# Sigmoid attention and a gated feed-forward block: separate transpose banks, a refitted load order, and paired seventh token tiles

## The chip, the cores and the metric

The kernel runs on one core of one Trainium2 chip. The metric is device time in microseconds (us) of one execution. The kernel before takes 422.9 us (median of three runs, 422.77 to 423.55). The names used below: PE is TensorE (PEld its weight loads), DVE is VectorE, ACT is ScalarE, POOL is GpSimd, SP is SyncE, which issues nearly all loads.

## The reference

```python
batch, n_heads, seq, head_dim = 8, 12, 448, 64        # q, k, v in float32, 0.1 * randn
scores = q @ k.T / sqrt(64) - log(448)
x = sigmoid(scores) @ v                                # 3584 tokens x 768
g = x @ w_gate                                         # 768 x 1536
h = g * sigmoid(g) * (x @ w_val)
out = h @ w_out                                        # 1536 x 768
```

## The kernel before

The kernel writes its work as a list of operations, each with an engine, an estimated duration and what it depends on. A list scheduler with a model of the loads then fixes the order of the instructions of every engine, in the program, before it runs. So an edit in one place can move instructions anywhere.

The attention is cut into 24 units of four heads (q, k and v: 448 KB each); three units make one batch entry. Per unit: cast q and k to bf16, transpose (on PE for units 0 to 5, by DMA after that), seven score bursts on a quarter array (64x64), seven sigmoids on ACT, the values products, copies to `xT`. The first three units (one batch entry, 21 sigmoids) run before there is feed-forward work. These are the parts that the change touches:

```python
ORDER = "v1 q2 q3 w0 q4 w1 w2 q5 w3 q6".split()   # order of loads; "q2" = q, k, v of unit 2, "w0" = first quarter of both weights
...
stt = [stg.tile([128, 2 * NS * D], FP32, tag=f"st{n}", name=f"st{n}") for n in range(slots["st"])]   # staging for loads
...
cast_qk(0, "q", None, [("DVE", 0, 4, 0), ("ACT", 4, NS, 0)])
tr_pe(0, 0, [("DVE", 0, 4), ("ACT", 4, NS)])       # one PSUM tile for both parts
...
cuts = [0, 5, NS] if i < QB else [0, NS]           # values product of units 0 to 2 in two parts
...
a = op("PE", 0.19 * JS, mm(w, nm, 0, JS), ...)     # first gate and value products in two parts, JS = 4
```

The output product h @ w_out of two token tiles e and o with the two halves of the inner dimension is done by seven products of six matmuls in place of eight (a Strassen-like scheme with sums on DVE). A group of two batch entries has seven token tiles of 128, so three pairs and one tile left over. Before, the seventh tile is computed the ordinary way:

```python
def f2_items(m):
    return [x for k in range(NS // 2) for x in f2_set(m, k)] + \
        [(1.0, lambda final, u=u: f2(m, u, final)) for u in (2 * NS - 2, 2 * NS - 1)]   # 12 matmuls a half-column
```

Of the kernel before, what the change touches and what calls it, by code (L numbers as in the profile page):

```python
# [27 lines left out]
class Op:  # L28
# [3 lines left out]
    def __init__(self, eng, dur, fn, deps=(), mode=("F", "F"), take=(), give=(), desc=(0, 0)):  # L32
        self.eng, self.dur, self.fn, self.mode = eng, dur, fn, mode
        self.deps = [d if isinstance(d, tuple) else (d, 0.0) for d in deps if d is not None]
        self.take = [Slot(t) for t in take]
        self.give = list(give)
        self.rank = self.t0 = self.t1 = None
        n, size = desc
        self.hold = n == 1792
        self.dma = 2.0 if n == 1792 else n / 16 * max(0.042, 0.0093 + size / 28700)  # L40
# [10 lines left out]
ORDER = "v1 q2 q3 w0 q4 w1 w2 q5 w3 q6".split()  # L51
# [7 lines left out]
VDMA = 24  # L59
VISSUE = 1.6  # L60
# [3 lines left out]
def list_schedule(ops, bufs, window):  # L64
# [34 lines left out]
    while left:  # L99
        later = []  # L100
        did = False
        for e, q in queues.items():
# [6 lines left out]
            if e == "PE" and now > 100 and mode == "Q":  # L109
                rs = [ready(o) for o in q[:NEAR] if o.mode[0] == mode]  # L110
                rs = [r for r in rs if r is not None and r <= now + STICK]
                soon = min(rs) if rs else None
# [41 lines left out]
def kernel(  # L154
# [55 lines left out]
    stt = [stg.tile([128, 2 * NS * D], FP32, tag=f"st{n}", name=f"st{n}") for n in range(slots["st"])]  # L210

    def wsum(j, c, n=1):

        x = (j - 1) * NH + c
        o = x % 4 * HW
        return stt[NEARLY + x // 4].bitcast(FP16)[:, o:o + n * HW]

# [75 lines left out]
    def load_v(i):  # L293

        b, r = divmod(i, QB)

        def fn():
            t = T["v16", i] = sb.tile([128, 2, NS, D], FP16, tag="v16", bufs=slots["v16"], name=f"v16_{i}")
            x = v[b][4 * r:4 * r + 4].rearrange("(a g) (p s) d -> a g p (s d)", a=2, s=NS)
            nc.gpsimd.dma_start(out=t[:, 0].rearrange("q s d -> q (s d)"), in_=x[0].rearrange("g p c -> (g p) c"))  # L300
            for g in range(2):
                nc.gpsimd.dma_start(out=t[64 - 64 * g:128 - 64 * g, 1].rearrange("q s d -> q (s d)"), in_=x[1, g])
        R["v16", i] = op("POOL", VISSUE, fn, take=["v16"], desc=(256, NS * D * 4))

# [40 lines left out]
    def tr_pe(i, n, parts=None):  # L345
# [4 lines left out]
        def fpe(s0, s1):  # L350
            def fn():
                if s0 == 0:
                    T["tr", i, n] = psum.tile([128, NS, 128], BF16, tag="TO", bufs=2, name="ps_tr")
# [6 lines left out]
        def fm(eng, s0, s1):  # L360
            def fn():
                if n == 0 and s0 == 0:
                    qkT_tile(i)
                cp(eng, T["qkT", i][:, n, s0:s1], T["tr", i, n][:, s0:s1])
            return fn
        for k, (eng, s0, s1) in enumerate(parts):
            a = op("PE", 0.06 * (s1 - s0), fpe(s0, s1), deps=[ins[min(k, len(ins) - 1)]],
                   take=["TO"] if s0 == 0 else [], give=R["cq", i][0].take if n and s1 == NS else [])
            if s0 == 0:
                bank = a.take  # L370
            m = op(eng, 0.1 + (0.53 if eng == "DVE" else 0.8) * (s1 - s0) / NS, fm(eng, s0, s1), deps=[a],
                   take=["qkT"] if n == 0 and s0 == 0 else [], give=bank if s1 == NS else [])
# [46 lines left out]
    def pv(i):  # L419
# [25 lines left out]
        cuts = [0, 5, NS] if i < QB else [0, NS]  # L445
# [15 lines left out]
    def f1(b, f):  # L461
# [30 lines left out]
        JS = 2 * (QB - 1)  # L492

        def product(w, nm, deps):
            deps = deps + R["w16", "w" + nm, c]
            if b or f:
# [3 lines left out]
            a = op("PE", 0.19 * JS, mm(w, nm, 0, JS), deps=xs[:JS] + deps, take=["G"])  # L500
            return op("PE", 1.14 - 0.19 * JS, mm(w, nm, JS),
                      deps=xs[:JS] + [(o, 0.19 * n) for n, (o, _) in enumerate(xs[JS:])] + [a]), a.take
# [12 lines left out]

    ev = [0]

    def f2(m, u, final=False):
        t, half = divmod(u, 2)
        end = m == B // 2 - 1 and t == NS - 1  # L520
        if end and half:
            w = DM // 4
            parts = [("A", slice(2 * w, 3 * w)), ("TO", slice(3 * w, 4 * w))]
        else:
            w = DM // 2
            parts = [("A" if final and u % 4 < 2 else "TO", slice(half * w, half * w + w))]
        a = [f2_part(m, u, final, end, n, *p) for n, p in enumerate(parts)]
        R.setdefault(("f2", m), []).extend(a)

    def f2_part(m, u, final, end, n, tag, cs):  # L530
        t, half = divmod(u, 2)
        w = cs.stop - cs.start

        def fpe():
            if half == 0:
                T["osb", m, t] = sb.tile([128, DM], FP32, tag="osb", bufs=slots["osb"], name=f"osb_{m}_{t}")
            if tag == "A":
                o = psum.tile([128, 2, 512], FP32, tag="A", bufs=2, name="ps_ol")[:, 0, 0:w]
            else:
                o = psum.tile([128, w], FP32, tag="TO", bufs=2, name="ps_o")  # L540
            T["o", m, u, n] = o
            for f in range(NF):
                nc.tensor.matmul(out=o, lhsT=T["hT", m][:, f, t * 128:(t + 1) * 128],  # L543
                                 rhs=wo16[:, f, cs], start=(f == 0), stop=(f == NF - 1))

        def fe():
            if half == n and not (end and n):
                nc.scalar.activation(out=T["osb", m, t][:, cs], in_=T["o", m, u, n], func=COPY, scale=HREC)
            else:
                nc.vector.tensor_scalar_mul(T["osb", m, t][:, cs], T["o", m, u, n], HREC)  # L550

        def fo(c, blocks, dma):
            def fn():
                for k in blocks:
                    bb, s = divmod(2 * t + k, NS)
                    rows = slice((2 * m + bb) * S, (2 * m + bb + 1) * S)
                    dma.dma_start(out=out[rows, c].rearrange("(p s) d -> s p d", s=NS)[s],
                                  in_=T["osb", m, t][64 * k:64 * k + 64, c])
            return fn
        a = op("PE", 1.95 * w / (DM // 2), fpe,  # L560
               deps=[(R["hT", 2 * m + 1, f], 0.16 * f) for f in range(NF)] + [R["wo16", f] for f in range(NF)],
               take=[tag] + (["osb"] if half == 0 else []))
        if half == 0:
            R["osb", m, t] = a.got("osb")
        e = op("ACT" if half == n and not (end and n) else "DVE", 0.1 + 0.35 * w / (DM // 2), fe, deps=[a], give=a.got(tag))
        R["o", m, u] = e
        give = R["osb", m, t] if half and (n or not end) else []
        if end and n:
            op("SP", 0.5, fo(cs, [0], nc.sync), deps=[e], give=give)
            op("ACT", 0.5, fo(cs, [1], nc.scalar), deps=[e])  # L570
        elif end:
            op("SP", 0.5, fo(cs, [0], nc.sync), deps=[e])
            if half:
                op("ACT", 0.5, fo(cs, [1], nc.scalar), deps=[e])
            else:
                op("SP", 0.5, fo(cs, [1], nc.sync), deps=[e])
        elif half == 1:
            op("SP" if final else "POOL", 1.1, fo(slice(0, DM), [0, 1], nc.sync if final else nc.gpsimd),
               deps=[e, R["o", m, u - 1]], give=give)
        return a  # L580
# [26 lines left out]

    def f2_set(m, k):

        e, o = 2 * k, 2 * k + 1  # L610
# [3 lines left out]
        def blk(t, r):  # L614
            return T["hT", m][:, r * NH:(r + 1) * NH, t * 128:(t + 1) * 128]

        def hs(f0, f1):
            bs = {x // S for t in (e, o) for x in (t * 128, t * 128 + 127)}
            return [(R["hT", 2 * m + b, f], 0.16 * (f - f0)) for b in bs for f in range(f0, f1)]

        def c(t, cols):
            return T["osb", m, t][:, cols]

        def start(final):
            full = [d for d, _ in hs(0, NF)]

            def s1():
                for n in (1, 2):
                    T["s", n, m, k] = sb.tile([128, NH, 128], FP16, tag=f"S{n}", bufs=slots["S"],
# [12 lines left out]
        def product(n, lhs, rhs, deps, final):  # L642
            tag = "A" if final and n % 2 else "TO"

            def fn():
# [4 lines left out]
                for x in range(NH):  # L650
                    nc.tensor.matmul(out=T["p", m, k, n], lhsT=lhs()[:, x], rhs=rhs(x),  # L651
# [8 lines left out]
        def store(t, deps, give, final):  # L660
            dma = nc.sync if final else nc.gpsimd

            def fn():
                for x in (0, 1):
                    bb, s = divmod(2 * t + x, NS)
                    rows = slice((2 * m + bb) * S, (2 * m + bb + 1) * S)
                    dma.dma_start(out=out[rows].rearrange("(p s) d -> s p d", s=NS)[s],  # L667
                                  in_=T["osb", m, t][64 * x:64 * x + 64])
            op("SP" if final else "POOL", 1.1, fn, deps=deps, give=give)

        def step1(final):
# [4 lines left out]
            def fn():  # L676
                for t in (e, o):
                    if final:
                        T["osb", m, t] = staging("osf")[:, 0:DM]
                    else:  # L680
                        T["osb", m, t] = sb.tile([128, DM], FP32, tag="osb", bufs=slots["osb"], name=f"osb_{m}_{t}")
# [8 lines left out]
        def step3(final):  # L690
# [3 lines left out]
            add("c11", 2, (e, lo), (e, lo), [C["u2"]])  # L694

# [4 lines left out]
        def step5(final):  # L700
# [3 lines left out]
            P[5].give = C["s1"].take  # L704

        def step6(final):
            product(3, lambda: blk(e, 1), lambda x: wo16[:, NH + x, hi], [C["s4"]], final)
            add("c12", 3, (e, hi), (e, hi), [C["u4"]])
            store(e, [C["c11"], C["c12"]], C["p1"].take[:1], final)
# [182 lines left out]
```

## Time and profile before

| | kernel before |
|---|---|
| time, span of the profiled run | 422.9 us, 421.4 us |
| PE busy | 412.1 us (98%) |
| DVE, ACT, POOL busy | 54%, 52%, 31% |
| PE full from | 48 us to the end |
| from PE's last matmul to the end of the span | 3.55 us (span less 416.70 + 1.15) |

The lines that carry the reading are in the prediction. Read them so: where PE is full, only the number of matmuls counts; where it is not full (here the first 48 us), follow the waits in order of time; at the end, count what comes after the last matmul.

### The profile page before, as it was taken

To read this page: it belongs to the slowest core of one execution; us is meant where nothing else is said; L and a number is where in the kernel's file an instruction comes from. 1 tells how busy PE (TensorE), PEld (TensorE's weight loads), DVE (VectorE), ACT (ScalarE), POOL (GpSimd) and SP (SyncE) were. 2 spreads that over 40 slices of the span, in tenths; PEclk is the share of its full clock that TensorE was granted. 3 is DMA by queue.
4 is the path that set the end of the run, shared out by engine and by line. 5 is a ranking of instruction groups with operands and counts; after the bars stand their busy time and mean duration, and the time that the engine had idled before them with its cause. 6 is when DMAs were issued, how large, how long until landed. Compare 5 with 4: busy or idle time off the path is not lost.

```text
span 421.4 us, 7959 instructions
## 1 busy us (share of the span) xinstructions
PE 412.1 (98%) x3215; PEld 208.0 (49%) x3217; DVE 229.5 (54%) x401; ACT 218.8 (52%) x292; POOL 130.0 (31%) x194
## 2 busy tenths in 40 slices
PE   8989899999999999999999999999999999999996
PEld 3444444444445554554554544545445545555564
DVE  3444444467676744554465564555455474673773
ACT  5997578766771155455645446544745542112000
POOL 1887845766331231414304314224100001000000
PEclk9999999999999999999999999999999999999999
DMA  8999979997871284474663745746301103021054
GB/s 273 379 376 374 375 208 340 308 321 209 221 230 54 75 207 91 146 178 106 165 165 76 185 56 195 176 87 188 59 2 37 39 2 75 2 75 35 4 148 116
DMA packets 64628, 66.97 MB, mean 159 GB/s; under 512 B 35536, under 2 KB 60752, under 8 KB 64592
## 3 DMA queue, kind: packets, MB, share of 16 engines
q1 hardware_dynamic: 62704, 59.29, 49.0%
q0 software_dynamic: 1728, 7.08, 6.5%
q8 instruction: 25, 0.41, 0.4%
q10 hardware_dynamic: 160, 0.10, 0.1%
q14 instruction: 11, 0.09, 0.1%
HBM read 47.19 MB, written 11.01 MB: 138 GB/s over the span
## 4 chain that ended last, share of the span: by engine, by line
PE 89%; DMA 9%; SPq 1%; POOL 0%; issue 0%; DVE 0%; POOLq 0%
PE ps_g L472 25%; PE ps_v L472 23%; PE ps_o L651 16%; PE ps_sc L397 8%; PE ps_pv L432 6%; DMA st<-in_moe_w_val_dram 4%; DMA st<-in_q_dram 4%; PE ps_ol L651 4%; PE ps_vl L472 3%; PE ps_o L543 2%; PE ps_ol L543 2%; SPq L261 1%; PE ps_tr L355 0%; POOL src L231 0%; DVE osb L550 0%
## 5 line engine op out<-in xcount | busy, mean ns | idle before, releaser
L414 ACT ACTIVATE pt<-ps_sc,sbiast 128x896 f16<-128x896 f32 x168 | 159.1, 1006 | 29.1 <-PE ps_sc L397 29.1
L472 PE MATMUL ps_g<-xT,wg 128*128 128x448 f16 x576 | 124.3, 353 | 0.5 <-DVE t L482 0.4
L478 ACT ACTIVATE s<-ps_g 128x448 f16<-128x448 f32 x96 | 52.2, 544 | 123.8 <-PE ps_g L472 122.8
L472 PE MATMUL ps_v<-xT,wv 128*128 128x448 f16 x504 | 109.7, 353 | 0.0
L482 DVE TENSOR_TENSOR t<-ps_g,s 128x448 f16<-128x448 f32 x96 | 59.9, 624 | 91.3 <-ACT s L478 91.0
L472 PEld LDWEIGHTS <-wg 128*128 128x128 f16 x576 | 54.7, 98 | 55.4 <-issue 8.1
L472 PEld LDWEIGHTS <-wv 128*128 128x128 f16 x576 | 52.3, 98 | 58.3 <-issue 15.9
L488 DVE SCALAR_TENSOR_TENSOR hT<-ps_v,t 128x448 f16<-128x448 f32 x84 | 52.4, 624 | 34.6 <-PE ps_v L472 33.6
L231 POOL CAST src<-st 128x896 bf16<-128x896 f32 (+1 forms) x43 | 39.8, 927 | 100.6 <-DMA st<-in_q_dram 67.2
L397 PE MATMUL ps_sc<-qkT 64*64 64x448 bf16 x672 | 51.3, 360 | 1.8 <-ACT pt L414 1.3
L231 POOL CAST v<-st 64x448 f16<-64x448 f32 (+1 forms) x72 | 41.4, 575 | 25.8 <-issue 15.7
L651 PEld LDWEIGHTS <-hT 128*128 128x128 f16 x360 | 35.2, 98 | 25.4
L667 POOL DMA_DIRECT2D out_dram<-osb x32 | 16.7, 526 | 90.4 <-DVE osb L656 90.4
L432 PE MATMUL ps_pv<-pt,v 64*64 64x448 f16 x672 | 37.1, 350 | 0.4 <-ACT pt L414 0.4
L229 DVE CAST xT<-ps_pv 128x448 f16<-128x448 f32 x40 | 23.5, 620 | 24.0 <-PE ps_pv L432 24.0
L656 DVE SCALAR_TENSOR_TENSOR osb<-ps_o,osb 128x384 f32<-128x384 f32 x56 | 30.2, 552 | 6.3 <-PE ps_o L651 6.3
L651 PE MATMUL ps_o<-wo,hT 128*128 128x384 f16 x168 | 31.9, 326 | 0.0
L397 PEld LDWEIGHTS <-qkT 64*64 64x64 bf16 x672 | 14.9, 105 | 31.1 <-issue 27.3
L432 PEld LDWEIGHTS <-v 64*64 64x64 f16 x672 | 19.6, 107 | 14.3 <-issue 3.4
L651 PE MATMUL ps_o<-st,s 128*128 128x384 f16 x120 | 22.8, 326 | 0.0
L651 PE MATMUL ps_o<-st,hT 128*128 128x384 f16 x120 | 22.8, 326 | 0.0
L651 PEld LDWEIGHTS <-s 128*128 128x128 f16 x144 | 14.1, 98 | 10.2
(45 smaller groups left out, 202.5 us busy)
## 6 DMA issues: line engine op xcount, KB each, us to landing
st<-in_q_dram SPq DMA_DIRECT2D x24, 448.0 KB, 4.3
st<-in_v_dram SPq DMA_DIRECT2D x24, 448.0 KB, 5.5
st<-in_k_dram SPq DMA_DIRECT2D x23, 448.0 KB, 4.8
out_dram<-osb POOLq DMA_DIRECT2D x36, 192.0 KB, 3.2
st<-in_moe_w_gate_dram SPq DMA_DIRECT2D x12, 384.0 KB, 9.1
st<-in_moe_w_val_dram SPq DMA_DIRECT2D x12, 384.0 KB, 8.8
st<-in_moe_w_out_dram SPq DMA_DIRECT2D x12, 384.0 KB, 6.8
out_dram<-st SPq DMA_DIRECT2D x16, 192.0 KB, 2.7
```

Of the source, the lines that this page charges most:

```text
L229: nc.vector.tensor_copy(out=o, in_=i)
L231: nc.gpsimd.tensor_copy(out=o, in_=i)
L397: nc.tensor.matmul(out=sc[64 * (g ^ a):64 * (g ^ a) + 64, a, 0:S].rearrange("k (s p) -> k s p", s=NS), lhsT=kT[r, s, 64 * g:64 * g + 64], ...
L414: nc.scalar.activation(out=pt, in_=T[("sc",) + key][:, :, 0:S], func=SIGM, bias=sb_t, scale=qkscale)
L432: nc.tensor.matmul(out=T["pv", i, a][64 * g:64 * g + 64, :], lhsT=T["v16", i][r, a, s, :], rhs=T["pt", i, s][r, a, :], start=(s == 0), sto ...
L472: nc.tensor.matmul(out=T[nm, b, f], lhsT=w[c][:, j, ff * 128:(ff + 1) * 128], rhs=T["xT", b, j], start=(j == 0), stop=(j == KC - 1))
L478: nc.scalar.activation(out=t, in_=T["g", b, f], func=SIGM)
L482: nc.vector.tensor_tensor(out=t, in0=T["g", b, f], in1=T["s16", b, f], op=MULT)
L488: nc.vector.scalar_tensor_tensor(out=T["hT", m][:, f, o * S:(o + 1) * S], in0=T["v", b, f], scalar=HSC, in1=T["t1", b, f], op0=MULT, op1=MULT)
L543: nc.tensor.matmul(out=o, lhsT=T["hT", m][:, f, t * 128:(t + 1) * 128], rhs=wo16[:, f, cs], start=(f == 0), stop=(f == NF - 1))
L651: nc.tensor.matmul(out=T["p", m, k, n], lhsT=lhs()[:, x], rhs=rhs(x), start=x == 0, stop=x == NH - 1)
L656: C[name] = op("DVE", 0.45, lambda: nc.vector.scalar_tensor_tensor(out=c(*dst), in0=T["p", m, k, n], scalar=HREC, in1=c(*other), op0=MULT, ...
```

## The change

Its intent: start the sigmoid row earlier, take away two holes before PE is full, and replace the four ordinary seventh tiles by two pairs, which takes 12 of 96 matmul equivalents away. Two groups share a pair: POOL copies the seventh tile of the first group (`keep`), so that it stays until the seventh tile of the second group is there.

```diff
-ORDER = "v1 q2 q3 w0 q4 w1 w2 q5 w3 q6".split()
+ORDER = "v1 q2 q3 w0 q4 w1 q5 w2 q6 w3".split()
-        self.dma = 2.0 if n == 1792 else n / 16 * max(0.042, 0.0093 + size / 28700)
+        self.dma = 2.0 if n == 1792 else n / 16 * max(0.042, 0.003 + size / 24600)
...
-    stt = [stg.tile([128, 2 * NS * D], FP32, tag=f"st{n}", name=f"st{n}") for n in range(slots["st"])]
+    stage = stg.tile([128, slots["st"], NST], FP32, tag="st", name="st")
+    stt = [stage[:, n] for n in range(slots["st"])]
+    kept = stage.bitcast(FP16)[:, NEARLY:, 4 * HW:].rearrange("p a (b t) -> p a b t", t=128)
...
-        cuts = [0, 5, NS] if i < QB else [0, NS]
+        cuts = [0, 2, 5, NS] if i < QB else [0, NS]
...
+            for j in range(0, KC, 2):        # first gate and value products in three parts
+                a = op("PE", 0.38, mm(w, nm, j, j + 2), ...)
...
+    def keep(m):
...
+            return lambda: nc.gpsimd.tensor_copy(
+                out=kept[:, 3 * r:3 * r + 3],
+                in_=T["hT", m][:, r * NH:(r + 1) * NH, (NS - 1) * 128:].rearrange("p (a b) t -> p a b t", b=2))
...
+        last = k == NS // 2
+        e, o = ((m - 1, NS - 1), (m, NS - 1)) if last else ((m, 2 * k), (m, 2 * k + 1))
...
-    tr_pe(0, 0, [("DVE", 0, 4), ("ACT", 4, NS)])
-    cast_qk(0, "k", None, [("DVE", 0, 3, 0), ("POOL", 3, NS, 1)])
-    tr_pe(0, 1, [("DVE", 0, 3), ("DVE", 3, NS)])
+    tr_pe(0, 0, [("DVE", 0, 4), ("ACT", 4, NS)], split=True)        # a bank for each part
+    cast_qk(0, "k", None, [("DVE", 0, 1, 0), ("DVE", 1, 3, 0), ("POOL", 3, NS, 1)])
+    tr_pe(0, 1, [("DVE", 0, 1), ("DVE", 1, 3), ("DVE", 3, NS)], tag="G")
...
-        return [x for k in range(NS // 2) for x in f2_set(m, k)] + \
-            [(1.0, lambda final, u=u: f2(m, u, final)) for u in (2 * NS - 2, 2 * NS - 1)]
+        return [(0.0, lambda final: keep(m))] * (1 - m % 2) + \
+            [x for k in range(NS // 2 + m % 2) for x in f2_set(m, k)]
```

Cut out: the old `f2` and `f2_part`, which go; the stores of the last pair, which are cut by half-columns and issued by SP and ACT; PE's fill matmuls at the start, which now read `wide` alone and no longer wait for the identity; and small changes of the scheduler's constants and of its order rules.

## The prediction

> **What bounds the kernel now.** I read the page first, then busy time by stretch, then the first 62 us in order of time, then the chain of work that ended last. The page's first lines, and of the stretches the two around the place where TensorE fills up and one late one (stretch, length, busy time of PE, PEld, DVE, ACT, POOL, granted clock, DMA share, GB/s):
>
> ```profile
> span 421.4 us, 7959 instructions
> PE 412.1 (98%) x3215; PEld 208.0 (49%) x3217; DVE 229.5 (54%) x401; ACT 218.8 (52%) x292; POOL 130.0 (31%) x194
> ```
>
> ```profile
> 36.00:48.00 12.00, 10.50 (x98) 4.92 (x97) 5.38 (x9) 7.74 (x10) 8.97 (x12) 1.00 1.06 375
> 48.00:60.00 12.00, 12.00 (x110) 5.49 (x107) 6.38 (x11) 8.24 (x12) 8.41 (x12) 1.00 0.79 231
> 350.00:400.00 50.00, 50.00 (x302) 27.22 (x300) 29.14 (x52) 9.19 (x18) 1.36 (x3) 1.00 0.16 40
> ```
>
> From 48 us to the end TensorE never waits: the list of waits on PE between 48 and 410 us comes back empty. There only the number of matmuls counts. Before 48 us other things set the pace, so I read that part in order of time (start, duration, engine, line, instruction, idle time before it and who ended it):
>
> ```profile
> 6.03 0.48 ACT L227 COPY qkT<-ps_tr 128x384 bf16<-128x384 bf16 x1 [1.40 <-DVE qkT L229]
> 6.99 7.51 ACT L414 ACTIVATE pt<-ps_sc,sbiast 128x896 f16<-128x896 f32 x8 [0.48 <-PE ps_sc L397]
> 14.98 11.99 ACT L414 ACTIVATE pt<-ps_sc,sbiast 128x896 f16<-128x896 f32 x13 [0.48 <-PE ps_sc L397]
> ...
> 31.05 1.29 PE L472 MATMUL ps_g<-xT,wg 128*128 128x448 f16 x6 [0.35 <-DVE t L482]
> ...
> 43.59 0.93 POOL L231 CAST src<-st 128x896 bf16<-128x896 f32 x1 [0.43 <-DMA st<-in_q_dram]
> 44.58 0.56 PE L355 MATMUL ps_tr<-idn,src 128*128 128x128 bf16 x7 [1.47 <-POOL src L231]
> ```
>
> Three things are to be seen. From 6.99 to 26.97 us ScalarE runs 21 sigmoids nearly back to back (7.51/8 = 0.94 us each); everything up to the first gate product hangs on when that row starts, and it has one hole of 0.48 us. At 31.05 PE waits for a PSUM bank. At 44.58 PE waits 1.47 us for the cast of unit 5's q, which waited for its load: the queue is full until 48 us (375 GB/s), and q5 stands behind six loads of weights.
>
> **What the Trainium skill says.** "PSUM — Partial Sum Buffer", Terms, says that two engines on one bank and quadrant at once is an error, so users of a bank have to be serialised. The trace agrees: ScalarE's copy of three transposes waits 1.40 us, until VectorE's copy from the same bank is through. "TensorEngine Tiling (Array Packing)", Key Properties: changing the tiling mode drains TensorE. The trace agrees: in the chain a six-matmul product takes 1.14 us, and 1.24 after a burst of 64x64 products. So I counted stretches of 64x64 work in the built programs: 81 before, 81 after. "TensorE: Matmul & The Clock Gate", Part 1, gives about 3.4 us of activity before the full clock; here the first fill matmuls load weights 0.43 us apart and later ones 0.21. "Perfetto Trace Analysis", Identifying the Most-Contended Engine, warns that matmul busy time misleads; therefore I work below with counts times pitch.
>
> **The change, part by part.**
>
> *Seventh token tiles.* Before, each of the four token groups computes it classically: 8 half-columns of 12 matmuls, 84 of 384 columns and 24 of 192. After, tiles of two groups make a pair with seven products of six: 2 x 42 = 84 of 384 columns. The chain gives the pitch:
>
> ```profile
> 378.20 1.95 PE ps_ol L543 x12
> 396.37 1.95 PE ps_ol L651 x12
> ```
>
> Both forms cost 1.95/12 = 0.1625 us a matmul. Before: 96 equivalents = 15.6 us; after 84 = 13.65. That is **-1.95 us**, all on PE while it is saturated. It adds 4 copies of 128x768 on POOL (0.82 us each by the weight casts; POOL is idle 69%), and some 8 sums (0.55 us) plus 14 scaled adds (0.55 us) on VectorE, about 12 us on an engine that idles 192 us: beside other work. In the built program the copies stand well ahead of their readers.
>
> *The end.* Before, the last piece is 192 columns: VectorE 0.36 us, then 48 KB stores. After, it is 384 columns and 96 KB stores on two queues:
>
> ```profile
> 417.89 0.36 DVE L550 TENSOR_SCALAR osb<-ps_o 128x192 f32<-128x192 f32 x1 [0.63 <-PE ps_o L543]
> ```
>
> ```profile
> out_dram<-osb SPq DMA_DIRECT2D x2, 96.0 KB, 2.3
> out_dram<-osb ACTq DMA_DIRECT2D x2, 48.0 KB, 2.0
> ```
>
> VectorE's add of 384 columns takes 0.55 (row of the scaled adds), so +0.19; landing +0.25. **+0.45 us.**
>
> *Separate banks for the first unit's transposes.* With its own bank ScalarE waits for TensorE alone (the built program shows this), not for VectorE's copy. The transposes it needs start about 4.9 to 5.1 us; with the drain the copy can start near 5.4 instead of 6.03. First sigmoid near 6.4 instead of 6.99: -0.6 us. *Values product in three parts:* a score burst can now stand between the parts, where before twenty products stood in front of the second score burst of unit 1 and made the 0.48 us hole: -0.5. Together the sigmoid row ends near 25.9 instead of 26.97, **-1.1 us**, if every input is there. I checked the loads: the last of unit 2 is in at 15.4, and its scores are not needed before 19; unit 4's k is cast by 28.74, needed near 28.8 (tight).
>
> *The first gate and value products* come in three parts, and ScalarE now takes the gate's sigmoid after one score sigmoid, not two. The bank wait at 31.05 should shrink or move; PE reaches the second gate product near 29.3 instead of 31.05, but one score burst (0.5 us) then comes after it rather than before. Net of the 1.1 above: **-0.15 us**.
>
> *Order of loads.* q5 goes ahead of w2, and q6 ahead of w3. One piece lands about every 1.05 us (casts of w2 at 36.87, 37.89, 38.95), an attention piece every 1.2. So q5 and k5 are cast by about 39, and PE needs them near 41: **the 1.47 us stall goes**. The price: w2 lands 3.6 us later. Its gate half would be cast near 43.5 and its value half near 46.4; my walk along the new PE order needs them near 46.6 and 49.6. w3 would be cast by 53.5 and 56.6, needed near 56.5 and 58. Margins are 1.4 to 3 us. So **-1.47 us**.
>
> The refitted load model and the earlier "stay with attention" rule only reorder; the count of mode changes is equal, at most one less in the saturated part: 0 to -0.2, taken as **-0.1**.
>
> Sum: -1.95 + 0.45 - 1.1 - 0.15 - 1.47 - 0.1 = **-4.3 us**. 422.9 - 4.3 = **418.6 us**, 1.0% faster.
>
> **The rivals.**
> 1. *Startup gain eaten by the loads.* Until 48 us the queue runs full, and no byte is removed. If PE comes 2.7 us earlier to weights that come 3.6 us later, the 1.47 us stall returns in front of w2 or w3, or at unit 4's transposes. For it: 375 GB/s, the tight k4. Against: margins of over 1 us. The time would then be 420 to 420.5.
> 2. *The end becomes VectorE's.* The last 168 matmuls (27.3 us) are now all output work, with 3 or 4 sums and 7 adds a pair, about 6 us of VectorE per 6.8 us of PE. If an add chain falls behind, PE waits for banks. Against: the three pairs before run just so from 400 to 413 us without a gap. Worth +0.5 to +1.
> 3. *A false dependency.* Staging becomes one tile, and the kept tiles lie in its slots. If readers of weight sums had to wait for POOL's copies, PE would stall in mid kernel. Against: in the built program PE's waits in the output products are of the same kinds and number as before (3 on POOL in both).
> 4. *Larger gain:* the earlier fill (its wait for the identity, built at 1.34, is gone; zeros are there at 1.13) brings the full clock earlier and the first transposes pass faster, another 0.2 to 0.4 us.
>
> **Range and chances.** The matmul count is sure to 0.1 us. The startup sum of 2.7 us I trust to about 1 us, more downwards; the end to 0.3. Rivals 1 to 3 lean slower. So 417.5 to 420.3 should hold it 8 times in 10. Faster by over 2% would need 414.4, some 4 us more than anything I find; slower by over 2% needs a new stall of 12 us in a saturated kernel. Chances: 0.02, 0.97, 0.01.
>
> **What would show each step.** Right: first sigmoid near 6.4 us and 21 of them without a hole until about 25.9; no PE wait on POOL's cast of q5 near 43; PE full from about 46; 12 output matmuls fewer in equivalents; last VectorE add of 0.55 us and some 4.0 us from the last matmul to the end (3.55 now). Wrong: PE idle before w2 or w3 products between 44 and 58 us, waits on VectorE among the last 168 matmuls, or PE waiting for POOL's kept copies. What would break the prediction is such a wait in the saturated part, where every microsecond counts in full.

## The result, and the profile after

The changed kernel is correct. It took 420.54 us (median of six runs, 419.33 to 421.38), the kernel before 422.88 (six runs, 422.58 to 423.55). The ratio is 0.9941, with a 95% interval of 0.9923 to 0.9959. A ratio here is the mean time of one kernel's fast runs over that of the other's of the same rounds, so not quite the ratio of the medians. It is faster by 0.6%, but 420.54 lies above the predicted range of 417.5 to 420.3, and 2.34 us were gained where 4.3 were expected.

The page's first two lines after, and the stretch in which PE fills up (columns as in the prediction):

```profile
span 419.0 us, 7945 instructions
PE 410.4 (98%) x3194; PEld 205.1 (49%) x3194; DVE 237.7 (57%) x420; ACT 217.5 (52%) x290; POOL 133.3 (32%) x196
```

```profile
36.00:48.00 12.00, 12.00 (x116) 5.76 (x114) 6.59 (x12) 8.67 (x11) 9.98 (x13) 1.00 1.06 376
```

The hole between 36 and 48 us is gone (10.50 before, 12.00 now). The first sigmoid, the sigmoid row and the way to the second gate product, in order of time:

```profile
5.35 0.48 ACT L231 COPY qkT<-ps_tr 128x384 bf16<-128x384 bf16 x1 [0.75 <-PE ps_tr L348]
6.31 3.70 ACT L408 ACTIVATE pt<-ps_sc,sbiast 128x896 f16<-128x896 f32 x4 [0.48 <-PE ps_sc L391]
10.52 6.39 ACT L408 ACTIVATE pt<-ps_sc,sbiast 128x896 f16<-128x896 f32 x7 [0.50 <-PE ps_sc L391]
17.50 9.25 ACT L408 ACTIVATE pt<-ps_sc,sbiast 128x896 f16<-128x896 f32 x10 [0.60 <-PE ps_sc L391]
...
29.50 0.56 PE L348 MATMUL ps_tr<-idn,src 128*128 128x128 bf16 x7 [0.68 <-POOL src L235]
...
30.70 0.56 PE L348 MATMUL ps_tr<-idn,src 128*128 128x128 bf16 x7 [0.26 <-POOL src L235]
31.10 1.30 PE L466 MATMUL ps_g<-xT,wg 128*128 128x448 f16 x6
```

ACT's copy now waits for PE alone, and the first sigmoid starts at 6.31, as predicted (6.4). But two new holes of 0.50 and 0.60 us stand in the row, which therefore ends at 26.75 (17.50 + 9.25), 0.2 us earlier than before and not 1.1. PE then waits 0.94 us for the casts of unit 4's q and k, which wait for their loads (the last part of that q landed at 28.36 us, its cast began at 28.51), and the second gate product starts at 31.10 where I had 29.3. Yet the stall that the new load order was to remove is gone. The cast and the transposes of unit 5's q:

```profile
38.42 0.93 POOL L235 CAST src<-st 128x896 bf16<-128x896 f32 x1 [0.46 <-DMA st<-in_q_dram]
...
42.81 0.55 PE L348 MATMUL ps_tr<-idn,src 128*128 128x128 bf16 x7
```

At the end, PE's last product, and DVE's last add:

```profile
413.66 1.14 PE L599 MATMUL ps_o<-st,hT 128*128 128x384 f16 x6
...
414.83 0.56 DVE L604 SCALAR_TENSOR_TENSOR st<-ps_o,st 128x384 f32<-128x384 f32 x1 [0.42 <-PE ps_o L599]
```

PE ends at 414.80, 3.05 us earlier than before (4.75 expected), and 4.2 us follow it (419.0 - 414.80; 3.55 before, 4.0 expected). So the mechanism of each part is visible. In the prediction's own terms, all that is missing is missing at the start: the row of sigmoids ends 0.85 us late (26.75 for 25.9), the second gate product starts 1.8 us late (31.10 for 29.3), and PE's end is late by no more than that (1.7 us, 4.75 - 3.05).

### The profile page after: what moved, and what is told of

Read it like the earlier page. It is cut to its first block, busy times and chain, and to the rows that moved or that the text cites. A ratio compares the mean times of both kernels' runs of the same rounds, so it can differ in the third digit from the quotient of the medians.

```text
span 419.0 us, 7945 instructions
## 1 busy us (share of the span) xinstructions
PE 410.4 (98%) x3194; PEld 205.1 (49%) x3194; DVE 237.7 (57%) x420; ACT 217.5 (52%) x290; POOL 133.3 (32%) x196
## 3 DMA queue, kind: packets, MB, share of 16 engines
q0 software_dynamic: 1632, 6.69, 6.3%
## 4 chain that ended last, share of the span: by engine, by line
PE 90%; DMA 6%; DVE 1%; ACT 1%; SPq 0%; issue 0%; POOL 0%; POOLq 0%
PE ps_g L466 26%; PE ps_v L466 23%; PE ps_o L599 18%; PE ps_sc L391 8%; PE ps_pv L426 7%; PE ps_ol L599 5%; DMA st<-in_k_dram 4%; PE ps_vl L466 3%; DMA st<-in_v_dram 3%; ACT pt L408 0%; SPq L265 0%; PE ps_tr L348 0%; DVE t L476 0%; DVE hT L585 0%; POOL src L235 0%
## 5 line engine op out<-in xcount | busy, mean ns | idle before, releaser
L599 PEld LDWEIGHTS <-hT 128*128 128x128 f16 x384 | 37.6, 98 | 27.2
L614 POOL DMA_DIRECT2D out_dram<-osb x34 | 17.7, 525 | 93.6 <-DVE osb L604 93.5
L604 DVE SCALAR_TENSOR_TENSOR osb<-ps_o,osb 128x384 f32<-128x384 f32 x63 | 34.0, 551 | 6.2 <-PE ps_o L599 6.2
L599 PE MATMUL ps_o<-st,s 128*128 128x384 f16 x138 | 26.2, 326 | 0.0
L599 PE MATMUL ps_o<-st,hT 128*128 128x384 f16 x138 | 26.2, 326 | 0.0
L599 PEld LDWEIGHTS <-s 128*128 128x128 f16 x168 | 16.4, 98 | 11.8
```

Source lines behind the costliest of these rows:

```text
L599: nc.tensor.matmul(out=T["p", m, k, n], lhsT=lhs()[:, x // 2, x % 2], rhs=rhs(x), start=x == 0, stop=x == NH - 1)
L604: C[name] = op("DVE", 0.45, lambda: nc.vector.scalar_tensor_tensor(out=c(*dst), in0=T["p", m, k, n], scalar=HREC, in1=c(*other), op0=MULT, ...
L614: dma.dma_start(out=out[rows, cols].rearrange("(p s) d -> s p d", s=NS)[s], in_=T[("osb",) + t][64 * x:64 * x + 64, cols])
```

## The experiments

My theories for what is missing: **J**, the loads land at other times in each execution, and the changed kernel's start hangs on them; **L**, unit 4's transposes wait for loads in every execution; **C**, the pairs' added work disturbs PE. The rival of J is **S**: something in the changed program makes its loads late every time.

### 1. The same kernels again

No edit. Kernels `a_...` are made from the changed kernel, `b_...` from the one before.

> The changed kernel once more, nothing edited. What is open: in its first profile the pieces of q, k and v landed up to 1.9 us later than in the kernel before (q4 cast at 28.5 us against 26.6), although the same bytes moved, and ScalarE's row of 21 sigmoids got two holes (0.50 and 0.60 us). Theory J (jitter: one of the 16 DMA engines is held up now and then, and a load lands when its slowest engine is through): this profile will have other landing times, q4's cast anywhere from 26.6 to 28.6 us, and the times scatter over some 2 us around 420.5. Rival S (something in the changed program makes the loads late every time): q4's cast again at 28.5 within 0.3 us and both holes again.

> The kernel before once more, for its profile. Theory J: its landings move too, q4's cast between 26.6 and 28.6 us; because its sigmoid row starts 0.7 us later it may hide more of it. Rival S: q4's cast at 26.6 within 0.3 us again, as in the first profile of it.

> The changed kernel a third time, as the measure for its neighbours on the chip. Theory J (landings and the opening of TensorE's clock differ from execution to execution, not from program to program): median between 419.3 and 420.6, scatter 1.2 to 2.1 us, and its profile shows other landing times than the first two. Rival S: 420.5 within 0.3 and q4's cast at 28.5 as in the first profile.

| run | us, median (all runs) | ratio to before, interval |
|---|---|---|
| first measurement | 420.54 (419.33 to 421.38) | 0.9941 (0.9923, 0.9959) |
| a_again | 419.35 (418.87 to 420.06) | 0.9911 (0.9895, 0.9927) |
| a_again2, on another chip than a_again | 419.94 (419.69 to 421.71) | 0.9933 (0.9913, 0.9953) |
| b_again (one run) | 423.49 | |

The sigmoid row of a_again, and its transposes of unit 4 with the second gate product:

```profile
6.23 10.19 ACT L408 ACTIVATE pt<-ps_sc,sbiast 128x896 f16<-128x896 f32 x11 [0.51 <-PE ps_sc L391]
16.63 9.25 ACT L408 ACTIVATE pt<-ps_sc,sbiast 128x896 f16<-128x896 f32 x10 [0.21 <-PE ps_sc L391]
...
28.59 0.56 PE L348 MATMUL ps_tr<-idn,src 128*128 128x128 bf16 x7 [0.64 <-POOL src L235]
...
29.86 0.56 PE L348 MATMUL ps_tr<-idn,src 128*128 128x128 bf16 x7 [0.33 <-POOL src L235]
30.26 1.30 PE L466 MATMUL ps_g<-xT,wg 128*128 128x448 f16 x6
```

This is the row that I had predicted: no hole but one of 0.21, and its end at 25.88 (25.9 predicted). The same program gave 26.75 in its first profile. What differs is set beside each other here, all from the profiles. "k of unit 1, first and last" is when the first and when the last of the 16 parts of that load landed, counted in the trace from the first landing of all; all other times count from the start of the span.

```
                         before  b_again  b_neworder | changed  a_again  a_again2
k of unit 1, first         4.05     3.89     4.07    |   4.09     3.73     3.90
k of unit 1, last          5.77     4.86     6.69    |   6.54     5.08     5.84
unit 4's q, first part    24.73    24.69    24.99    |  24.82    24.51    24.81
unit 4's q, last part     26.43    27.21    27.46    |  28.36    27.46    26.98
unit 4's q cast starts    26.58    27.36    27.61    |  28.51    27.60    27.12
TensorE's full clock from  5.57     5.76     6.89    |   4.98     4.75     6.38
first sigmoid              6.99     7.03     7.16    |   6.31     6.23     6.69
row of 21 sigmoids ends   26.97    27.00    27.50    |  26.75    25.88    26.32
unit 4's transposes wait                             |   0.94     0.97     0.17
second gate product                                  |  31.10    30.26    29.73
time of that execution   423.29   423.49   422.41    | 420.82   420.06   419.76
```

The first part of k of unit 1 lands within 0.4 us of the same moment everywhere. Its last part comes 1.0 to 2.6 us after it, and that differs from execution to execution, in the kernel before as in the changed one. For unit 4's q it is 1.7 to 3.5 us. A load is usable only when its last part is there: the cast of that q starts 0.14 to 0.15 us after it in all six. Rival S falls: a_again and a_again2 show other landings with the same program, and the kernel before can be late too. In the changed kernel the time follows the start of the second gate product closely: time less that start is 389.72, 389.80 and 390.03 us. Between these three executions the start moves by 1.37 us and the time by 1.06. The first profile caught it late. Only the profiled execution of each measurement can be looked at so. And a_again and a_again2 ran on different chips: whether the chip has a part in their medians was not tested.

A second source shows in the first PE work. Ten transposes at 4.6 us took 0.91 us in the first profile, 0.90 in a_again and 1.25 in a_again2, and the first sigmoid came at 6.31, 6.23 and 6.69. "TensorE: Matmul & The Clock Gate", Part 1, of the Trainium skill says that the clock opens by a free-running window, so at another moment in each run. The clock records, which the trace files keep, agree (table above). In the eight profiles of kernels with the split banks in which the full clock came after 6.3 us, the first sigmoid starts at 6.69 to 6.85 us; in the seven in which it came by 5.1 us, at 6.17 to 6.41. That is some 0.5 us.

### 2. The order of loads, undone and alone

```diff
 # a_oldorder, in the changed kernel          # b_neworder, in the kernel before: the reverse edit
-ORDER = "v1 q2 q3 w0 q4 w1 q5 w2 q6 w3".split()
+ORDER = "v1 q2 q3 w0 q4 w1 w2 q5 w3 q6".split()
```

> The changed kernel with the old order of loads (w2 ahead of q5, w3 ahead of q6). My prediction gave the new order 1.47 us, all of it a TensorE wait on the cast of q5: then this one takes 1.5 us longer than the changed kernel (422.0). Rival (the order only moves a wait that TensorE would make up elsewhere, because the bytes limit the start anyway): within 0.5 us of the changed kernel.

> The kernel before with nothing but the new order of loads. Prediction: 1.5 us less than the kernel before (421.4), the TensorE wait of 1.47 us at 44.6 us gone. Rival: the wait comes back in front of the products of the third weight quarter (44 to 58 us), and the time stays within 0.5 us of the kernel before.

Measured on one chip with a_again: a_oldorder 421.60 us (420.75 to 421.69), 2.25 more than a_again; b_neworder 422.01 (421.87 to 422.41), 1.14 less than the kernel before (423.15; ratio 0.9973, 0.9959 to 0.9986). In b_neworder the wait on unit 5's q is gone from the list of waits, and PE is full between 36 and 48 us (12.00), although its row ended 0.5 us later than in the other profiles of the kernel before (table above). Its stretch from 36 to 48 us:

```profile
36.00:48.00 12.00, 12.00 (x130) 5.80 (x126) 6.04 (x10) 9.09 (x12) 9.84 (x13) 1.00 1.06 377
```

From the second gate product to the end of the span it took 388.93 us, the kernel before 390.35 and 390.52. So the order alone is worth 1.1 us by the times and 1.4 to 1.6 us in that stretch; 1.47 was predicted. The way back is no clean measure. PE's waits after 60 us in a_oldorder (line waited for: us in total, times, longest):

```profile
PE ps_g L466 <- DVE t L476: 1.2, 2, 0.9
PE ps_sc L391 <- ACT pt L408: 1.1, 1, 1.1
PE ps_v L466 <- DVE hT L482: 0.2, 1, 0.2
```

Of these 2.5 us (0.74 in a_again) 0.93 is the wait near 120 us that section 6 explains, and 1.09 is a wait of one score burst at 60.44 us. The scheduler, given the old order, also placed other instructions elsewhere: by line and tile, 170 of 3192 matmuls stand in another place than in a_again. That it causes the new waits is not shown. It did so in b_neworder too (426 of 3215), but there PE has no wait after 60 us, as in the first profile of the kernel before. So b_neworder is the better test of the step, though not a perfectly clean one.

### 3. Loads made lighter, transposes made later

a_halfw0 and a_halfv keep every instruction in its place and move fewer bytes. Their outputs are wrong, which doesn't matter for the times. a_m7 and a_m15 tell the scheduler to expect the transposes of unit 3 and later 0.7 or 1.5 us later (those of unit 3 kept their place among their neighbours, those of unit 4 moved).

```diff
 # a_halfw0: each load of the first weight quarter moves one of its two row blocks
-                out=T[nm, c, j2],
+                out=T[nm, c, j2][:, 0:1 if c == 0 else 2],
 # a_halfv: v of units 0 to 4 moves one of its two halves, and the cast reads that half twice
-                    out=T["st_" + nm, i][:, :, s0:s1]...
+                    out=T["st_" + nm, i][:, 0:1 if nm == "v" and i < 5 else 2, s0:s1]...
 # a_m7 (a_m15: 1.5)
-MARGIN = 0.0
+MARGIN = 0.7
-                   deps=[(ins[min(k, len(ins) - 1)], -MARGIN if i > QB else 0.0)],
+                   deps=[(ins[min(k, len(ins) - 1)], -MARGIN if i >= QB else 0.0)],
```

> The changed kernel with the same instructions in the same order; only the six loads of the first weight quarter move half their bytes (the result is wrong on purpose). Everything behind them, unit 4's q and k first, lands some 3 us earlier. Theory L (the missing microsecond of my startup sum is the wait of unit 4's transposes for their loads, 0.97 us in the repeated profile): both waits go, the second gate product starts near 29.3 us instead of 30.26, and the time is 1.0 us under the changed kernel's 419.35 of the last session, about 418.4. Rival A (ScalarE's sigmoid row paces that stretch anyway, the wait only fills a gap): the time stays at 419.3.

> The changed kernel with the same instructions in the same order; only the loads of v of units 0 to 4 move half their bytes (the result is wrong on purpose), so that what stands behind them lands up to 2.4 us sooner. Theory L (loads cost the start its missing gain): no hole in the sigmoid row after unit 1, no wait of unit 4's transposes, second gate product near 29.3 us, and the time 0.7 to 1.0 us under the changed kernel beside it, with less scatter. Rival (a wait further on takes it back): within 0.3 us of it.

> The changed kernel with the load model of the scheduler told to expect unit 4's and later transposes 0.7 us later. In the built program the transposes of unit 4's q now stand behind the last value parts, those of its k three groups further on. Theory L: the waits shrink from 0.97 us to under 0.3 and the time falls by 0.6 to 1.0 us against the changed kernel, to about 418.5. Rival A: no gain, 419.3, because scores of unit 4 then reach ScalarE later.

> The same with 1.5 us: the transposes of unit 4's q stand behind the second gate product and a burst of scores. Theory L: no wait is left even where loads land late, so the time is as with 0.7 us, 418.4, and scatters less than the changed kernel (which scattered 2.05 us over six runs and 1.2 over four). Rival A: slower than with 0.7 us by 0.3 us or more.

| run | us, median (all runs) | ratio, interval |
|---|---|---|
| a_halfw0 | 419.82 (418.59 to 420.75) | 0.9909 (0.9885, 0.9933) |
| a_m7 | 419.99 (419.51 to 420.87) | 0.9919 (0.9899, 0.9940) |
| a_m15 | 420.96 (420.13 to 421.88) | 0.9942 (0.9920, 0.9965) |
| a_halfv, beside a_again2 | 419.95 (418.84 to 420.80) | 0.9922 (0.9904, 0.9940) |

a_halfv's way to the second gate product:

```profile
27.96 0.55 PE L348 MATMUL ps_tr<-idn,src 128*128 128x128 bf16 x7
28.35 0.54 PE L466 MATMUL ps_v<-xT,wv 128*128 128x448 f16 x2
28.73 0.55 PE L348 MATMUL ps_tr<-idn,src 128*128 128x128 bf16 x7
29.14 1.30 PE L466 MATMUL ps_g<-xT,wg 128*128 128x448 f16 x6
```

The mechanism of theory L is confirmed: with lighter loads both waits vanish in both kernels, the row has no hole over 0.21 us, and PE is there at 29.14 (29.3 predicted; 29.61 in a_halfw0, whose clock opened late, at 6.73 us). But the time did not follow. The median equals that of a_again2 (419.94), and six runs still scatter over 1.96 us. So L is a miss as an account of the time. Two readings remain. The loads ahead of the first v (k of unit 0, q and k of unit 1) and the clock's opening were not touched and still scatter. And a part is given back: from the second gate product to the end of the span a_halfv took 388.36 us and a_halfw0 388.39, the changed kernel 387.90, 387.94 and 388.27, with PE waiting for DVE after 60 us for 0.94 and 1.0 us against 0.54, 0.74 and 0.85. What makes all of the 2 us of scatter stays open.

a_m7 has no wait at the transposes in its profile, but PE then waits 0.26 us for the bank of the gate product; in a_m15 that wait is 0.65 us, since the second gate product stands straight behind the first values. Neither ran beside the changed kernel on its chip, nor did a_halfw0; by their ratios a_m7 is no better than the changed kernel, and a_m15, 0.97 us over a_m7 beside it, no better either. The rival's "no gain" holds; the way is another than it named, since the transposes trade their wait for one at the bank.

### 4. The first unit: one bank, two parts

```diff
 # a_nosplit
-    tr_pe(0, 0, [("DVE", 0, 4), ("ACT", 4, NS)], split=True)
+    tr_pe(0, 0, [("DVE", 0, 4), ("ACT", 4, NS)])                    # and k's partition as before
 # a_twopart
-        cuts = [0, 2, 5, NS] if i < QB else [0, NS]
+        cuts = [0, 5, NS] if i < QB else [0, NS]
```

> The changed kernel with the first unit's transposes back in one bank for q and the old partition for k. Prediction: ScalarE's copy waits for VectorE's again and the first sigmoid starts near 7.0 us instead of 6.2 to 6.85 (seen in six profiles), the row of 21 sigmoids ends 0.6 us later, and the time is 0.6 us over the changed kernel. Rival (in most executions the loads of units 1 to 4 set the end of the row and the start behind it, not the first sigmoid): the row starts later but the time differs by less than 0.3 us.

> The changed kernel with the values product of the first units in two parts again (five slices, then two). Prediction: twenty products stand ahead of a burst of unit 1's scores, the hole of 0.48 us in the sigmoid row is back, and the time is 0.5 us over the changed kernel. Rival (loads set the end of that stretch): less than 0.2 us.

a_nosplit took 419.66 us (419.30 to 420.52, ratio 0.9905), a_twopart 419.63 (419.14 to 419.90, ratio 0.9901), both as fast as the changed kernel or faster. ACT's copy and row in a_nosplit, then the row in a_twopart:

```profile
5.69 0.48 ACT L231 COPY qkT<-ps_tr 128x384 bf16<-128x384 bf16 x1 [1.03 <-DVE qkT L233]
6.66 19.52 ACT L408 ACTIVATE pt<-ps_sc,sbiast 128x896 f16<-128x896 f32 x21 [0.48 <-PE ps_sc L391]
```

```profile
6.47 7.50 ACT L408 ACTIVATE pt<-ps_sc,sbiast 128x896 f16<-128x896 f32 x8 [0.48 <-PE ps_sc L391]
14.36 11.86 ACT L408 ACTIVATE pt<-ps_sc,sbiast 128x896 f16<-128x896 f32 x13 [0.39 <-PE ps_sc L391]
```

Each shows its mechanism: with one bank the copy waits for DVE again (1.03 us), and with two parts the hole after eight sigmoids is back (0.39). Yet the rows end at 26.18 and 26.22 us, within the 25.88 to 26.75 of the changed kernel. Worth of the split banks in the start of the row: 0.35 to 0.43 us (6.66 against 6.31 and 6.23; the full clock came at 4.64, 4.98 and 4.75 us in these), not 0.6, and worth in time: none that can be seen. Here the rivals hold. With one bank the row of 21 has no hole at all. The profiled execution of a_nosplit was the slowest of its six (420.52): in it PE waits 1.07 us for DVE at 119.76 us, which section 6 explains.

### 5. The seventh tiles the old way, and another end

a_classic7 and a_classic7b (the same kernel twice) take back the old `f2` for the seventh tiles and drop `keep`; all else is as changed. a_tail cuts the very last product in two:

```diff
 # a_classic7, a_classic7b
-        return [(0.0, lambda final: keep(m))] * (1 - m % 2) + \
-            [x for k in range(NS // 2 + m % 2) for x in f2_set(m, k)]
+        return [x for k in range(NS // 2) for x in f2_set(m, k)] + \
+            [(1.0, lambda final, u=u: f2(m, u, final)) for u in (2 * NS - 2, 2 * NS - 1)]
 # a_tail: step 7 of the last pair as two products of 192 columns, each with its add and its stores
+            if end:
+                return last_halves(final)
```

> The changed kernel with the seventh token tiles computed the old way, by 96 products of twelve, and the old ending; the rest as changed. My prediction: 1.95 us of matmuls come back and 0.45 us at the end go, so 1.5 us more than the changed kernel, about 420.9. Rival: the additional VectorE and GpSimd work of the pairs costs TensorE waits, then the difference is under 1 us; or the end costs less than I said, then it is nearer to 2 us.

> The seventh tiles the old way once more. Measured from the start of the second gate product to the end of the execution, its first profile took 388.63 us, those of the changed kernel 387.90, 387.94 and 388.27: the pairs gain 0.6 us there and not the 1.5 of my prediction. Expected again: 388.6 within 0.3, and no TensorE wait at 119 us.

> The changed kernel with its very last product cut in two halves of 192 columns, each with its own add and 48 KB stores. TensorE ends 0.18 us later (12 x 0.096 against 6 x 0.1625), the last add takes 0.36 us instead of 0.56, and the stores land some 0.4 us sooner after it (3.15 us from the last add to the end before, 3.6 after). Expected: from TensorE's last matmul to the end 3.6 us instead of 4.15, net 0.4 us less. Rival: the two additional stores queue up behind the earlier ones and the gain is under 0.1 us.

a_classic7 took 420.72 us (ratio 0.9937, 0.9915 to 0.9959), a_classic7b 420.26 (0.9927, 0.9914 to 0.9939). Two things follow.

First, these two kernels hold everything of the change but the pairs, and gain 0.63% and 0.73% of 423 us, that is 2.7 and 3.1 us. Their spans say the same: 418.5 and 418.6 us against 421.4 and 421.6 of the kernel before. My sum for those parts was 1.1 + 0.15 + 1.47 + 0.1 = 2.8 us. So these parts were right as a sum.

Second, from the second gate product to the end they took 388.63 and 388.92 us, the changed kernel 387.90, 387.94 and 388.27. The pairs gain 0.74 us there (mean 388.78 less 388.04), not 1.5: the rival of a_classic7 ("under 1 us") holds. By the times alone nothing of it is seen: the mean ratio of three measurements of the changed kernel is 0.9928, that of these two 0.9932, and they did not run beside each other.

The end of a_classic7 has the lines of the kernel before (last matmul to end 418.5 - 414.92 = 3.6 us); the changed kernel has 4.2, 4.14 and 4.24. So the end costs 0.64 us, not 0.45: the add takes 0.20 more (0.56 against 0.36), and from there to the end of the span it is 3.61, 3.55 and 3.64 us against 3.15 before, 0.45 where I had 0.25. a_tail was a miss: 420.13 us (ratio 0.9910), which cannot be told from the changed kernel, and in its profile 4.5 us follow the last matmul (418.8 - 414.33), more than the 4.2 that it was to cut. The issuing of its stores (SPq and ACTq lines are the time in which a queue issues) and its last add:

```profile
411.57 4.28 SPq L614 DMA_DIRECT2D out_dram<-st  x5
411.57 4.58 ACTq L614 DMA_DIRECT2D out_dram<-st  x5
...
414.36 0.36 DVE L682 SCALAR_TENSOR_TENSOR st<-ps_ol,st 128x192 f32<-128x192 f32 x1
```

Each queue issues five stores in a row, which lasts until 415.85 and 416.15, over a microsecond past the end of the last add (414.72). The smaller pieces are ready sooner and stand in line behind the issues of the others, as the rival said.

### 6. The copies that are kept

In the changed kernel PE waits for DVE at 119 to 120 us, in each of its three profiles (0.24, 0.44 and 0.55 us); neither profile of the old tiles has that wait. There, in the changed kernel's first profile:

```profile
117.56 0.75 DVE L582 TENSOR_TENSOR s<-s,hT 128x768 f16<-128x768 f16 x1
117.85 1.14 POOL L541 COPY st<-hT 128x768 f16<-128x768 f16 x1
118.23 1.17 DVE L585 TENSOR_TENSOR hT<-hT 128x768 f16<-128x768 f16 x1
...
119.99 1.29 PE L466 MATMUL ps_g<-xT,wg 128*128 128x448 f16 x6 [0.24 <-DVE t L476]
```

The sums take 0.75 and 1.17 us (0.54 or 0.55 alone) beside POOL's cast of k, which runs until 117.90, and its copy, and the copy takes 1.14 (0.82 alone). "SBUF — State Buffer", Who interferes with whom, of the Trainium skill says that a VectorE instruction with two inputs in SBUF contends with a GpSimd instruction that reads SBUF. This agrees.

```diff
 # a_keepact, a_keepact2, a_keepact3 (one kernel); a_km7 adds the edit of a_m7
-            return lambda: nc.gpsimd.tensor_copy(
+            return lambda: nc.scalar.copy(
-            R["kept", m, r] = op("POOL", 0.95, fn(r), ...)
+            R["kept", m, r] = op("ACT", 0.85, fn(r), ...)
```

> The changed kernel with the four copies of 128x768 (hidden rows kept for the pairs) on ScalarE instead of GpSimd. In the profiles of the changed kernel VectorE's two sums beside the first copy take 0.75 and 1.17 us where they take 0.55 elsewhere, and TensorE then waits 0.24 to 0.44 us for VectorE at 119 us; with the old seventh tiles that wait is absent. Theory C (GpSimd's copy and VectorE's sum hold each other up): the sums take 0.55 again, the wait at 119 us is gone, the time 0.3 us less. Rival V (it is just the added VectorE work): the wait stays.

> The copies on ScalarE once more, beside the changed kernel on one chip. Theory C (GpSimd's copies hold VectorE's sums up and TensorE then waits 0.24 to 0.54 us at 119 us): 0.4 to 0.8 us less than the changed kernel beside it. Rival: the gain of a_keepact was landing luck, then within 0.2 us of it.

> The pairs with the copies on ScalarE. Theory C (the collision with GpSimd ate part of the 1.95 us, the longer end 0.64 of them): from the second gate product to the end it takes 387.6 within 0.2 again (387.54 and 387.67 so far), 1.0 us less than the old form beside it, and the time is 1.0 to 1.3 us less. Rival: the old form is as fast within 0.5 us, so the pairs are worth nothing once their end is paid for.

> Copies on ScalarE, and the transposes of unit 4 placed later as in a_m7. If the waits of the transposes (0.2 to 1.0 us) and the wait at 119 us add up, it takes 0.3 to 0.8 us less than a_keepact2, about 418.2. Rival: the transposes only trade their wait for one on VectorE's gate product (0.26 us in a_m7), then it equals a_keepact2 within 0.3 us.

| run | us, median (all runs) | ratio, interval |
|---|---|---|
| a_keepact | 418.82 (418.29 to 419.53) | 0.9885 (0.9865, 0.9904) |
| a_keepact2, beside a_again2 | 419.08 (418.67 to 419.92) | 0.9905 (0.9889, 0.9920) |
| a_keepact3, beside a_classic7b | 419.26 (418.67 to 419.51) | 0.9899 (0.9886, 0.9913) |
| a_km7, beside a_again2 | 420.14 (418.57 to 420.38) | 0.9919 (0.9900, 0.9937) |

Copies on ACT are faster than either form beside which they ran: 0.86 us less than the changed kernel on one chip (419.94), 1.0 less than the old tiles on another (420.26), and on three chips about 1% less than the kernel before. From the second gate product to the end they took 387.54, 387.67 and 387.42 us. The wait at 119 us is gone in all three profiles. But theory C holds only in part. The same place in a_keepact:

```profile
115.73 0.92 DVE L579 TENSOR_TENSOR s<-hT 128x768 f16<-128x768 f16 x1
...
117.57 0.90 DVE L585 TENSOR_TENSOR hT<-hT 128x768 f16<-128x768 f16 x1
...
118.76 1.14 PE L599 MATMUL ps_o<-wo,hT 128*128 128x384 f16 x6
...
119.73 1.30 PE L466 MATMUL ps_g<-xT,wg 128*128 128x448 f16 x6
```

Two of the sums are still slow, now beside POOL's casts of q, k and v (the kernel before has sums of 0.73 and 1.17 us beside such casts, too, and PE does not wait there). The three sums ahead of that gate product (L579, L582, L585) settle what the wait is. With the old tiles they take 2.20 us together, in both profiles:

```
                       changed  a_again  a_again2  a_nosplit | a_keepact  a_keepact2  a_keepact3
the three sums            2.47     2.66      2.77       3.29 |      2.36        2.67        2.44
what they take over 2.20  0.27     0.46      0.57       1.09 |      0.16        0.47        0.24
PE's wait after them      0.24     0.44      0.55       1.07 |      none        none        none
```

With the copies on POOL, PE's wait is what the sums take over 2.20 us, to within 0.03 us, in these four profiles and in seven further ones. But the copy is not all of it. In a_again and a_again2 the first sum alone takes 1.12 and 1.23 us; it starts when POOL's cast of k has begun and the copy has not. With the old tiles it started 0.16 and 0.01 us ahead of that cast and took 0.55. So part of the wait hangs on when a load landed, with the pairs or without. On ACT the copies leave 0.16 to 0.47 us of it. What takes PE's wait away is that the scheduler placed an output product ahead of the gate product, so that PE has work while DVE is late. Of the 0.5 us (388.04 less 387.54) I estimate, from the means of the middle row, 0.14 for the shorter sums (0.43 less 0.29) and 0.29 for the place of that product; no run tests them apart. a_km7 met neither expectation: it took 1.06 us more than a_keepact2 beside it, though its six runs overlap with those (418.57 to 420.38). Its transposes have no wait, but a new wait for DVE (0.66 us near 98 us) stands in its profile.

## Why the prediction was wrong

- **The range.** The median was 420.54, the range ended at 420.3. The step that failed first is "I checked the loads", with its "if every input is there". I took the landing times of one profile as fixed. They move: unit 4's q was cast from 26.58 to 28.51 us in six profiles. The profile that I had worked from was the earliest of these. With the changed kernel tied to the loads, PE waits up to 0.97 us for unit 4's transposes, and the second gate product started at 31.10, 30.26 and 29.73 us, not at 29.3. From there to the end of the span the prediction implies 387.8 us (421.4 - 4.3 - 29.3), and it took 387.90, 387.94 and 388.27. So the start is what failed. That the rest fits is partly luck: the pairs gained less than expected (next point) and the other parts more, since without the pairs it took 388.63 and 388.92 where the prediction implies 389.3. The first measurement was late; the repeats, 419.35 and 419.94, lie in the range. With lighter loads the waits go and PE is there at 29.14, but the median of the times does not fall, so the cause of the whole scatter stays open. Rival 1 of the prediction had the time (420 to 420.5) and, as one of two places, the right one ("at unit 4's transposes", "the tight k4"); its other one, a stall in front of the later weights, came in no profile of the changed kernel. I gave the rival too little.
- **Seventh tiles, -1.95 us.** The count and the pitch hold. Mis-sized is "beside other work" for the 12 us on DVE: its sums are held up beside POOL's casts and copies, and PE waits 0.24 to 0.55 us at 119 us where it did not before (in part by the moment at which a load lands, section 6). With the old tiles as measure, the pairs gain 0.74 us with their end. 1.95 - 0.64 (end) - 0.41 (mean of the three waits) = 0.90; 0.16 stays unexplained. With the copies on ACT, an output product moved ahead and no such wait, they gain 1.24 (388.78 less 387.54) against 1.95 - 0.64 = 1.31.
- **The end, +0.45 us.** 0.64 measured. The add is as predicted (0.20 for 0.19); mis-sized is the way from the last add to the end with 96 KB stores, 0.45 for 0.25.
- **Separate banks and three parts, -1.1 us.** Right in a_again (row end 25.88), but 0.65 in a_again2 (clock late) and 0.2 in the first profile (loads late). Undoing either one costs no time that five rounds can see, so it was not right to count them in full.
- **First gate and value products, -0.15 us.** The bank wait at 31.05 is gone in the changed kernel. PE was at the second gate product at 29.73 to 31.10, at 29.14 with light loads (29.3 predicted).
- **Load order, -1.47 us.** Right: -1.14 alone by the times, -1.4 to -1.6 in its stretch, the wait gone, no wait on later weights. The sum of all start parts, 2.8 us, was right too: 2.7 and 3.1 without the pairs.
- **Rivals 2 to 4.** No wait on DVE in the last 168 matmuls, and none on the kept copies themselves (rivals 2 and 3 did not come). Rival 4, the earlier clock, comes in some executions and not in others (full clock at 4.98, 4.75 and 6.38 us, against 5.57 and 5.76 in the kernel before).

All told, 2.8 + 0.74 = 3.5 us would be the gain by the parts. The three measurements gave 2.5, 3.8 and 2.8 us (by ratio, of 423). What was missing in the first is, as far as its profile shows, the late start.

## What to carry to other kernels

Before an early stage is tied closer to its loads, profile the kernel twice or more and take the spread of the landing times as the margin: one profile shows one throw of the dice. Work that is "free" on VectorE or GpSimd has to be looked at where it falls: here the two slowed each other down (0.55 us became up to 1.23), and TensorE waited for the slowed one. And with a scheduler in between, an ablation is clean only if the order of the instructions stays the same: change bytes or an engine, and compare the orders before the times.

## What the Trainium skill lacked or had wrong

- "DMA: Bandwidth & Descriptors" has no figure for how much the 16 parts of one load drift apart on hardware queues. Here the last part of one early load landed 0.97 to 2.62 us after the first in six profiles, and by another amount in each execution of the same program.
- "SBUF — State Buffer", Who interferes with whom, says that the loser of the shared ports is fully blocked. Here a sum that takes 0.55 us alone took 0.64 to 1.23 beside a GpSimd copy or cast. The one that started at 118.23, with the copy running until 118.99, ended at 119.40, 0.41 us later: less than its whole length. So full blocking is not shown, unless the span recorded for GpSimd is too long.
- "TensorE: Matmul & The Clock Gate", Part 1, gives a scatter of plus or minus 500 ns for the opening of the clock. Here it is wider: in the 17 profiles of the changed kernel and its variants the first fill matmul starts at 1.19 us, and the full clock came at 4.64 to 7.15 us.
- "TensorE: Matmul & The Clock Gate", Part 1, calls the ramp under 1% of a typical span. So it is here, but its scatter moved the first sigmoid of one program from 6.23 to 6.69 us, half of what separates two versions of a tuned kernel (0.86 us between a_again2 and a_keepact2).
